# Attention into a multiplicative feed-forward network on one core: a half chunk's numerator and division placed elsewhere, and stores put behind the last transpose

## The chip, the cores and the metric

The kernel runs on one core of one Trainium2 chip. The metric is the device time of one execution in microseconds; the time before is the median of three runs. The engines are TensorE (PE in the profile; its weight loads are PEld), VectorE (DVE), ScalarE (ACT), GpSimd (POOL) and SyncE (SP). Transfers are issued by POOL (loads, and most stores), SP (transposes, and some stores) and ACT (the last stores).

## The reference

Eight batches of eight heads, 576 positions, head size 64. The first part is linear attention with cosine weights, the second a network that multiplies two projections.

```
phi(x) = concat(relu(x) * cos(theta), relu(x) * sin(theta))        # theta = pi/2 * position / 576
kv  = phi(k)^T v           z = sum over positions of phi(k)        # per batch and head
x   = (phi(q) kv) / (phi(q) z + 1e-6)                              # 4608 rows of 512
out = ((x w1) * (x w2)) w3 w_out                                   # w1, w2: 512 x 1024; w3: 1024 x 1024; w_out: 1024 x 512
```

## The kernel before, in words

**Tiles.** A batch has five chunks c of positions: 0 to 3 with 128 rows and chunk 4 with 64 (the "half chunk"). The 4608 rows of x make nine tiles t of 512 rows, so a tile takes chunks of two batches: tile 6 has batch 5's chunks 1 to 3 and batch 6's chunk 0; tile 7 has batch 6's chunks 1 to 4 and batch 7's half chunk; tile 8 has batch 7's chunks 0 to 3.

**The order is written out by hand.** `PLAN` (lines 26 to 259) is a text in which each line is a row of steps, and the loop at lines 1180 to 1183 issues them from the top down. Every engine, and every issuer of transfers, takes its own instructions in this order, one after another; a step that waits holds all that its engine has behind it. The words that matter here (b is the batch, c the chunk, t the tile; the last letter is the engine: V VectorE, A ScalarE, G GpSimd):

- `f t` is the next step of tile t's first stage, the products with w1 and w2 (`ffn_groups`, line 696, and for tiles 6 to 8 `fast_units`, line 832). For tiles 2 to 5 the same generator goes on with the output products (`seven_products`, line 1010). `o t` is the next step of the output products of tiles 6 to 8.
- `q b c n` makes the features of a query chunk: the cosine half on VectorE (L513), the sine half of the first n heads on ScalarE (L518), the other heads on VectorE (L521). `qd b c` transposes them into `qpT` by a DMA that SP issues (L542).
- `n b c` is the numerator with its denominator: eight products of 65 columns on TensorE (L605) into a pair of PSUM banks, `pnum`. `d b c` divides: `den` with the 1e-6 (L617 on ScalarE where the step says A, L619 on VectorE otherwise), a reciprocal (L620) and the product `xblk` (L621), both on VectorE. There are two pairs of `pnum` banks until the word `more` (line 193); from then on one, so a numerator waits until the division before it has read the bank. `xd b c` transposes `xblk` into its place in the tile's `xT` by a DMA that SP issues (L643).
- `xs t i` are four sums of x blocks for tiles 6 to 8 (L830); `h t p V` combines two partial results into abT (L890); `s t i V` are sums of abT blocks for the output products (L1008). All are on VectorE.
- `st` stores the oldest finished pair of 128-row blocks of the output through POOL, `ss` through SP. `sg` and `sx` do what `st` does behind a gate: a one-element copy on POOL (L432) that reads some tile and so waits until this tile is there. `sg` reads the newest `asb`, a copy that only the tiles before 6 make; `sx` reads the first column of the block that was transposed last in the plan's order. All later POOL work stands behind the gate.

A pair to be stored goes out as two or four transfers, depending on where its rows lie.

**Tiles 6 to 8** make their first stage with seven products in place of eight, in 14 steps for units 0 and 1. The steps are, as (unit, product): (0,1), (0,7) and (0,6) for each half, (0,4), (0,2), (0,5), (1,1), (0,3), (1,6), (1,7), (1,2), (1,4), (1,5), (1,3). For tile 6 these are the words `f 6` of lines 195, 197 to 208 and 211; lines 203 to 208 are (0,3) to (1,5). VectorE and ScalarE read the banks after each product: L862, L866, L869 and L877 are ScalarE's copies, L872, L881 and L884 VectorE's sums and products.

**The output products** of tiles 2 to 7 are also seven in place of eight (L1019): A11 B11 into a bank `u`, then s3 t3 into a bank `w`, and later products that are added into the same banks after ScalarE (L1030) or VectorE (L1027) has read them. In tiles 2 to 5 the product s2 t2 goes into `u` behind the copy of C11 by ScalarE, and s4 B22 goes into `u` behind VectorE's addition to C22. The second product into w's bank waits likewise for the copy of C22.

Around the edits:

```
136..141   f 3 twice, then: tile 3's last products (L705, abT L774), then its output products
186..196   tile 5's output products, with batch 6's numerators and divisions
202..217   tile 6's first stage and output products, with batch 7's numerators
218..237   tile 7, with batch 7's last divisions (line 225) and transposes (line 226), and the stores
```

Of the kernel before, what the change touches and what calls it, by code (L numbers as in the profile page):

```python
# [134 lines left out]
f 3  # L135
f 3
f 3; xd 3 2
f 3; lg 6 v 0; n 4 2; n 4 3; d 4 2 A; q 5 0 8; xd 4 1; q 5 3 8
f 3
f 3; xd 4 0; lx 6 q 0; lg 6 q 1  # L140
f 3; l 6 v 1; lg 6 k 0; v 6 1 G
f 3
f 3
# [42 lines left out]
f 5; q 7 0 8  # L186
f 5
f 5
f 5; n 6 0; xd 5 2; n 6 4; d 6 0 A; d 6 4 A; v 7 0 A
f 5  # L190
f 5; lg 7 k 1; lg 7 v 1; n 6 2; d 6 2 A; xd 6 0; v 7 4 G; xd 6 4
f 5
f 5; more
# [8 lines left out]
f 6; q 7 1 4; xd 6 2; sg; kv 7  # L202
f 6; q 7 3 8; h 6 0 V; s 6 3 V
f 6
f 6
f 6
f 6
f 6; n 7 4; h 6 1 V; qd 7 1
o 6; s 6 2 V; d 7 4 A
o 6  # L210
f 6; s 6 1 V; qd 7 3; s 6 4 V; n 7 3; xd 6 1; gx 0; d 7 3 A
o 6; sx; xd 6 3
# [13 lines left out]
f 7; xd 7 1  # L226
f 7; ss
f 7
f 7; h 7 1 V; s 7 2 V; xs 8 1 V; sg; s 7 1 V
o 7  # L230
f 7; s 7 4 V
o 7
# [982 lines left out]
```

## Time and profile before

| What | Value |
|---|---|
| time, median of 3 runs (lowest to highest) | 240.03 us (239.41 to 242.28) |
| the profiled execution's own time | 241.31 us |
| its span, first to last instruction | 239.5 us |
| TensorE busy | 230.4 us, 96% |
| VectorE, ScalarE, GpSimd busy | 193.1, 134.7, 88.6 us |
| granted TensorE clock | 1.000 |
| bytes moved | 40.51 MB, mean 169 GB/s |

The rows of the timeline are: start in us, duration in us, engine, line, operation, output tile <- input tiles, shapes, x how many instructions are merged in the row, and in brackets the engine's idle time ahead of the row with what ended it. A row is cut at the end of the window that was asked for. In the rows of the chain of waits stand start, duration, engine, tile, line and count. The rows of the table of windows give, for a stretch, the busy time of PE, PEld, DVE, ACT and POOL with the instructions in brackets, then the granted clock, the share of the DMA engines' time and GB/s. A row of DMA issues gives tiles, issuer, kind, count and the median time from issue to landing in us; "DMA to landing us min/median/max" is the same for all issues of one line.

### The profile page before, as it was taken

To read this page: it belongs to the slowest core of one execution; us is meant where nothing else is said; L and a number is where in the kernel's file an instruction comes from. 1 tells how busy PE (TensorE), PEld (TensorE's weight loads), DVE (VectorE), ACT (ScalarE), POOL (GpSimd) and SP (SyncE) were. 2 spreads that over 40 slices of the span, in tenths; PEclk is the share of its full clock that TensorE was granted. 3 is DMA by queue.
4 is the path that set the end of the run, shared out by engine and by line. 5 is a ranking of instruction groups with operands and counts; after the bars stand their busy time and mean duration, and the time that the engine had idled before them with its cause. 6 is when DMAs were issued, how large, how long until landed. Compare 5 with 4: busy or idle time off the path is not lost.

```text
span 239.5 us, 6014 instructions
## 1 busy us (share of the span) xinstructions
PE 230.4 (96%) x2316; PEld 170.6 (71%) x2316; DVE 193.1 (81%) x448; ACT 134.7 (56%) x250; POOL 88.6 (37%) x163
## 2 busy tenths in 40 slices
PE   8899999999999999999999999999999899999993
PEld 3479544475974596698668857984889788978872
DVE  6984595968888977999989479997979898894782
ACT  2754314597665833776556445767579437627730
POOL 8653878680903324130342212502271231920000
PEclk9999999999999999999999999999999999999999
DMA  6999999999999999999599997999988763999304
GB/s 190 196 197 198 167 192 170 197 196 196 178 192 152 134 155 194 177 138 192 71 156 181 193 217 98 122 185 193 145 142 203 107 186 69 231 297 265 112 16 160
DMA packets 86013, 40.51 MB, mean 169 GB/s; under 512 B 49632, under 2 KB 83424, under 8 KB 85984
## 3 DMA queue, kind: packets, MB, share of 16 engines
q0 software_dynamic: 39024, 24.65, 70.0%
q1 hardware_dynamic: 46672, 15.28, 39.1%
q8 instruction: 18, 0.29, 0.5%
q10 hardware_dynamic: 288, 0.20, 0.3%
q14 instruction: 11, 0.09, 0.1%
HBM read 38.80 MB, written 9.44 MB: 201 GB/s over the span
## 4 chain that ended last, share of the span: by engine, by line
PE 59%; DMA 26%; POOL 6%; DVE 3%; issue 2%; SPq 1%; ACT 1%; DVEq 0%; POOLq 0%; ACTq 0%
PE ffnps L705 23%; PE ffnps L1019 11%; PE ffnps L849 8%; DMA qs<-in_q_dram 7%; DMA kf<-in_k_dram 6%; PE ffnmore L849 6%; DMA w2b<-in_moe_w_dram 5%; DMA xT<-xblk 4%; PE pnum L605 3%; PE ffnps L789 3%; PE pnum L570 3%; DMA early<-in_moe_w_out_dram 3%; POOL early L420 2%; DMA qpT<-qp 2%; PE ffnps L951 1%
## 5 line engine op out<-in xcount | busy, mean ns | idle before, releaser
L705 PE MATMUL ffnps<-xT,w1b 128*128 128x256 bf16 (+2 forms) x320 | 51.5, 294 | 0.2
L705 PE MATMUL ffnps<-xT,w2b 128*128 128x256 bf16 (+2 forms) x320 | 51.5, 294 | 0.0
L705 PEld LDWEIGHTS <-w1b 128*128 128x128 bf16 x320 | 28.8, 98 | 12.1 <-issue 0.8
L705 PEld LDWEIGHTS <-w2b 128*128 128x128 bf16 x320 | 28.7, 98 | 11.7
L621 DVE TENSOR_TENSOR xblk<-pnum,den 128x512 bf16<-128x512 f32 (+1 forms) x38 | 26.3, 691 | 2.1 <-DVE den L620 0.2
L768 ACT CAST asb<-ffnps 128x512 bf16<-128x512 f32 x24 | 14.0, 584 | 19.1 <-PE ffnps L705 17.3
L518 ACT ACTIVATE kp<-kf,sinv 128x512 bf16<-128x512 bf16 (+5 forms) x33 | 21.1, 663 | 0.8 <-DMA kf<-in_k_dram 0.8
L1019 PEld LDWEIGHTS <-abT 128*128 128x128 bf16 x192 | 18.6, 98 | 3.6 <-DVE abT L774 0.6
L518 ACT ACTIVATE qp<-qs,sinv 128x512 bf16<-128x512 bf16 (+4 forms) x29 | 18.0, 643 | 3.5 <-issue 1.7
L774 DVE TENSOR_TENSOR abT<-asb,ffnps 128x512 bf16<-128x512 bf16 x24 | 16.1, 678 | 4.8 <-PE ffnps L705 4.0
L534 POOL COPY va<-vs 128x512 bf16<-128x512 bf16 (+1 forms) x15 | 9.9, 666 | 23.7 <-DMA vs<-in_v_dram 23.7
L605 PEld LDWEIGHTS <-qpT 128*128 128x128 bf16 x320 | 14.4, 98 | 5.9 <-issue 1.5
L432 POOL COPY seen<-asb 128x1 bf16<-128x1 bf16 x16 | 3.9, 246 | 35.9 <-ACT asb L768 18.9
L605 PE MATMUL pnum<-kvs,qpT 128*128 128x65 bf16 x304 | 15.4, 194 | 1.6 <-DVE xblk L621 1.3
L758 DVE TENSOR_TENSOR abT<-asb,ffnps 128x512 bf16<-128x512 bf16 x16 | 10.9, 684 | 6.6 <-PE ffnps L705 5.6
L1030 ACT COPY osb<-ffnps 128x512 f32<-128x512 f32 x16 | 9.2, 582 | 11.9 <-PE ffnps L1019 10.3
L789 PE MATMUL ffnps<-w34b,abT 128*128 128x512 bf16 x64 | 15.6, 379 | 0.0
L513 DVE TENSOR_SCALAR kp<-kf,cosv 128x512 bf16<-128x512 bf16 (+1 forms) x40 | 15.4, 397 | 0.2 <-DMA kf<-in_k_dram 0.2
L1019 PEld LDWEIGHTS <-s 128*128 128x128 bf16 x144 | 13.7, 98 | 1.9 <-DVE s L1008 0.3
L751 ACT CAST asb<-ffnps 128x512 bf16<-128x512 f32 x16 | 9.3, 583 | 9.5 <-PE ffnps L705 9.5
L490 PE MATMUL ffnps<-early,turned 128*128 128x512 bf16 x64 | 14.3, 379 | 0.0
L513 DVE TENSOR_SCALAR qp<-qs,cosv 128x512 bf16<-128x512 bf16 (+1 forms) x34 | 12.0, 373 | 1.6 <-DMA qs<-in_q_dram 1.5
(163 smaller groups left out, 484.4 us busy)
## 6 DMA issues: line engine op xcount, KB each, us to landing
kf<-in_k_dram POOLq DMA_DIRECT2D x7, 320.0 KB, 7.9
early<-in_moe_w_dram POOLq DMA_DIRECT2D x16, 128.0 KB, 5.5
out_dram<-osb SPq DMA_DIRECT2D x8, 256.0 KB, 3.4
vs<-in_v_dram POOLq DMA_DIRECT2D x6, 320.0 KB, 6.0
kf<-in_k_dram POOLq DMA_DIRECT2D x7, 256.0 KB, 7.5
qs<-in_q_dram POOLq DMA_DIRECT2D x5, 320.0 KB, 6.1
qs<-in_q_dram POOLq DMA_DIRECT2D x6, 256.0 KB, 6.7
vs<-in_v_dram POOLq DMA_DIRECT2D x6, 256.0 KB, 7.7
```

Of the source, the lines that this page charges most:

```text
L490: nc.tensor.matmul(acc[:, :], lhsT=w3T[:, lc, :], rhs=woutb[:, lc, :], start=(lc == 0), stop=(lc == 7))
L513: nc.vector.tensor_scalar(out=dst[:R, c, :, 0:D], in0=rows[:R], scalar1=0.0, scalar2=cosv[:R, at:at + 1], op0=ALU.max, op1=ALU.mult)
L518: nc.scalar.activation(out=dst[:R, c, 0:n, D:F], in_=rows[:R, 0:n], func=ACTF.Relu, scale=sinv[:R, at:at + 1], bias=0.0)
L605: nc.tensor.matmul(nt[:, h // 4, ds((h % 4) * 65, 65)], lhsT=qpT[:, h, ds(at, 128)], rhs=kvs[:, h, :], start=True, stop=True)
L621: nc.vector.tensor_tensor(out=xblk[rows, g0:g0 + ng], in0=n4[:, :, :, 0:D], in1=den[rows, 0:ng].unsqueeze(3).to_broadcast([R, ng, 4, D]), ...
L705: nc.tensor.matmul(out, lhsT=w[:, kc, ts(jc, 128)], rhs=x[:, kc, tok], start=(first and kc == 0), stop=(kc == 3), skip_group_check=not first)
L758: nc.vector.tensor_mul(out=abT[:, ts(pair, 2), ts(half, 256)], in0=asb[:].rearrange("p (i n) -> p i n", i=2), in1=bT[:, :].rearrange("p (i ...
L768: nc.scalar.copy(out=asb[:], in_=aT[:, :])
L774: nc.vector.tensor_mul(out=abT[:, jc, :], in0=asb[:], in1=bT[:, :])
L789: nc.tensor.matmul(ops[:, :], lhsT=abT[:, jc, ts(ms, 128)], rhs=w34b[:, jc, :], start=(jc == 0), stop=(jc == 7))
L849: nc.tensor.matmul(into[:, ts(i, 256)], lhsT=w[:, kc, ts(2 * u + i, 128)], rhs=a[:, kc, :], start=(first and i == 0 and kc == 0), stop=(i ...
L1019: nc.tensor.matmul(into[:, ts(ms, 256)], lhsT=a[:, kc, ts(ms, 128)], rhs=b[:, kc, :], start=(first and ms == 0 and kc == 0), stop=(ms == 1 ...
```

## The change

Six lines of the plan become others; no function is touched.

```
-f 3; lg 6 v 0; n 4 2; n 4 3; d 4 2 A; q 5 0 8; xd 4 1; q 5 3 8
+f 3; lg 6 v 0; n 4 2; n 4 3; d 4 2 A; xd 4 1
 f 3
-f 3; xd 4 0; lx 6 q 0; lg 6 q 1
+f 3; q 5 0 8; q 5 3 8; xd 4 0; lx 6 q 0; lg 6 q 1
...
-f 5; n 6 0; xd 5 2; n 6 4; d 6 0 A; d 6 4 A; v 7 0 A
-f 5
+f 5; n 6 0; xd 5 2; d 6 0 A; v 7 0 A
+f 5; n 6 4; d 6 4 A
...
 f 6
+f 6; n 7 4; d 7 4 A
 f 6
 f 6
-f 6
-f 6; n 7 4; h 6 1 V; qd 7 1
-o 6; s 6 2 V; d 7 4 A
+f 6; h 6 1 V; qd 7 1
+o 6; s 6 2 V
...
-f 7; h 7 1 V; s 7 2 V; xs 8 1 V; sg; s 7 1 V
+f 7; h 7 1 V; s 7 2 V; xs 8 1 V; sx; s 7 1 V
```

1. Lines 138 and 140: the features of batch 5's chunks 0 and 3 are issued two lines later, behind tile 3's last pair of products and the first half of its first output product.
2. Lines 189 and 190: numerator and division of batch 6's half chunk are issued one step of tile 5's output products later; the copy `v 7 0` on ScalarE then comes ahead of the half chunk's `den`.
3. Lines 205 to 209: numerator and division of batch 7's half chunk are issued behind step (1,7) of tile 6, where the numerator stood behind (1,5) and the division behind the first output product and the sum `s 6 2`.
4. Line 229: the store that was gated by the newest `asb` is gated by the block transposed last in the plan's order, `xd 7 1` of line 226. The gate holds what POOL has behind it: this store (two transfers), the store of line 233 (four) and that of line 237 (two).

## The prediction

> **What bounds the kernel now.** I read the page's busy rows first, then the last steps of the chain of waits, then TensorE's timeline for rows that state an idle time, and around each of these the timelines of the other engines.
>
> ```profile
> span 239.5 us, 6014 instructions
> PE 230.4 (96%) x2316; PEld 170.6 (71%) x2316; DVE 193.1 (81%) x448; ACT 134.7 (56%) x250; POOL 88.6 (37%) x163
> ...
> 230.06 1.73 PE ffnps L951 x8
> ...
> 233.97 1.76 PE ffnps L951 x16
> ```
>
> TensorE (PE) is busy 96% of the span, and its products stand at the end of the chain, up to 235.73. So the change is worth what it takes from PE's idle time, and nothing else. From 65 us on, four rows of PE name an idle time and its releaser; I quote each with the row ahead of it.
>
> ```profile
> 124.51 0.49 PE L1019 MATMUL ffnps<-w34b,abT 128*128 128x256 bf16 x3
> 125.35 0.72 PE L1019 MATMUL ffnps<-w34b,abT 128*128 128x256 bf16 x5 [0.35 <-DVE abT L774]
> ...
> 168.26 0.42 PE L605 MATMUL pnum<-kvs,qpT 128*128 128x65 bf16 x8
> 168.96 0.42 PE L605 MATMUL pnum<-kvs,qpT 128*128 128x65 bf16 x8 [0.28 <-DMA qpT<-qp]
> ...
> 189.05 1.04 PE L1019 MATMUL ffnps<-early,s 128*128 128x256 bf16 x8
> 189.92 1.04 PE L849 MATMUL ffnps<-va,w2b 128*128 128x256 bf16 x8
> 191.85 0.42 PE L605 MATMUL pnum<-kvs,qpT 128*128 128x65 bf16 x8 [0.90 <-DVE xblk L621]
> 192.11 1.03 PE L1019 MATMUL ffnps<-early,s 128*128 128x256 bf16 x8
> ...
> 214.31 1.04 PE L1019 MATMUL ffnmore<-w34b,abT 128*128 128x256 bf16 x8
> 215.62 0.61 PE L849 MATMUL ffnps<-xT,w1b 128*128 128x256 bf16 x4 [0.28 <-DMA xT<-xblk]
> ```
>
> The bracket counts from the modelled end of a pipelined product. What is lost is counted better from starts: eight products of 256 columns take 0.87 (189.05 to 189.92), a numerator takes 0.26 (191.85 to 192.11). So 125.35 was due at 124.51 + 3/8 x 0.87 = 124.84 (0.51 lost), 168.96 at 168.52 (0.44), 191.85 at 190.79 (1.06), 215.62 at 215.18 (0.44). Together 2.45 us, 1.0% of the time: even the whole of it lies within the 2% that a measurement of this kernel can tell from no change. The four edits aim at these four waits, one each. What counts is what is late next.
>
> **Edit 1, two query features of batch 5 behind tile 3's last product.** Nothing is added or removed. Before, VectorE sat until the query load had landed, made both cosine halves, and only then multiplied the last abT for which PE waits.
>
> ```profile
> 123.97 1.33 ACT L518 ACTIVATE qp<-qs,sinv 128x512 bf16<-128x512 bf16 x2 [1.68 <-issue]
> 123.98 0.72 DVE L513 TENSOR_SCALAR qp<-qs,cosv 128x512 bf16<-128x512 bf16 x2 [0.67 <-DMA qs<-in_q_dram]
> 124.62 0.67 DVE L774 TENSOR_TENSOR abT<-asb,ffnps 128x512 bf16<-128x512 bf16 x1
> 125.22 1.05 ACT L1030 COPY osb<-ffnps 128x512 f32<-128x512 f32 x2
> 125.91 1.04 PE L1019 MATMUL ffnps<-early,s 128*128 128x256 bf16 x8
> ```
>
> After, L774 starts at 123.98 at the latest, where VectorE was free for the features, ends 0.67 later, and the product at 124.84 waits no more. But the sine halves are in ScalarE's order too, and the new line still puts them ahead of the copy of C11, which comes with the next `f 3`. ScalarE waits for the same load, copies C11 from 125.22 to about 125.8 (half of the 1.05 row, each copy overlapping the next), and the product at 125.91 accumulates into the bank that this copy reads. PE would now be there at 125.91 - 0.51 = 125.40 and waits until about 125.85 to 125.95. **Worth 0**; from both sides: -0.51 if that bank does not hold it, +0.1 if the copy's release is slow. The features' transposes on SP stand 15 lines further on in the plan; xd 4 1, which moves ahead of the features in the plan, is on SP and behind a division that is done in either order.
>
> **Edit 2, batch 6's half chunk one step on.** PE runs the 0.87 step first, so the transposed query that it waited for at 168.96 has landed when the numerator comes at 169.39. No instruction is added.
>
> ```profile
> 169.94 0.69 DVE L621 TENSOR_TENSOR xblk<-pnum,den 128x512 bf16<-128x512 f32 x1
> 173.29 1.43 DVE L1027 TENSOR_TENSOR early<-ffnps,early 128x512 f32<-128x512 f32 x2
> 174.78 1.03 PE L1019 MATMUL ffnps<-w34b,s 128*128 128x256 bf16 x8
> ```
>
> VectorE's order does not change by this edit (division of chunk 0, of chunk 4, addition, division of chunk 2, two additions), and the first division starts at 169.94 and the last two additions end at 173.29 + 1.43 = 174.72, with a fifth of a microsecond of idle time between. The product at 174.78 adds into the bank that the last of these additions reads. PE comes 0.44 earlier to the numerator of chunk 2, which needs chunk 0's bank (169.94 + 0.69 = 170.63, so a pause of some 0.2), and again 0.2 earlier to 174.78, where it waits for VectorE. **Worth 0**; -0.44 if VectorE runs ahead after all, +0.1 if the chunk's den, now behind another copy on ScalarE, delays the division.
>
> **Edit 3, batch 7's half chunk three steps sooner.** Before, numerator 7 4 was issued right ahead of tile 6's first output product, its division behind six VectorE instructions, and numerator 7 3 needs the same single bank.
>
> ```profile
> 185.15 1.09 ACT L866 COPY kf<-ffnmore 128x512 f32<-128x512 f32 x2
> 185.30 1.04 PE L849 MATMUL ffnps<-xT,w1b 128*128 128x256 bf16 x8
> 186.88 1.29 DVE L872 TENSOR_TENSOR s<-ffnmore,vs 128x512 bf16<-128x512 f32 x2 [0.61 <-PE ffnmore L849]
> 190.12 0.69 DVE L1008 TENSOR_TENSOR s<-abT,s 128x1024 bf16<-128x1024 bf16 x1
> 190.73 0.19 DVE L620 RECIPROCAL den<-den 64x8 f32<-64x8 f32 x1
> 191.02 0.68 DVE L621 TENSOR_TENSOR xblk<-pnum,den 64x512 bf16<-64x512 f32 x1
> 191.63 1.27 DVE L884 TENSOR_TENSOR abT<-asb,ffnps 128x512 bf16<-128x512 bf16 x2
> 196.72 0.75 DVE L830 TENSOR_TENSOR va<-xT 128x512 bf16<-128x512 bf16 x2
> 197.61 0.60 PE L849 MATMUL ffnmore<-va,q0f 128*128 128x256 bf16 x4
> ```
>
> After: numerator at 185.30, ScalarE's den behind its two copies (185.15 + 1.09 = 186.24) to about 186.3, VectorE free since 186.88 - 0.61 = 186.27, so reciprocal 186.31, division 186.60 (0.29 later, as 190.73 to 191.02), so the sums L872 start at 186.60 + 0.61 = 187.21 (0.61 as 191.02 to 191.63) instead of 186.88. The s of 190.12 then ends at 190.81 + 0.33 = 191.14, and L884 follows at once, at 191.06 instead of 191.63: VectorE gains **0.57**, the pause filled. PE issues numerator 7 3 at 190.79 without a wait and the product with s at about 191.2, not 192.11: 0.9 gained there. But down the line PE needs x sums that VectorE makes in unbroken order from 191.63 on: the second L830 ended at 196.72 + 0.75 = 197.47, and the product that reads it came at 197.61. That moves by VectorE's 0.57, so of PE's 0.9 about **0.6** stays. Bounds: 0 (the division meets other work) to -1.06 (the whole wait).
>
> **Edit 4, `sg` to `sx`.** The old gate read an asb of tile 5, long there, so nothing held the stores. The new gate reads the last transposed x block, 7 1, and all later stores of POOL stand behind it: two, four and, from line 237, two.
>
> ```profile
> 202.70 3.12 POOL L683 DMA_DIRECT2D out_dram<-osb  x6 [0.28 <-issue]
> 207.16 2.99 SPq L643 DMA_TRANSPOSE xT<-xblk  x1
> ...
> xT<-xblk SPq DMA_TRANSPOSE x1, 2.7
> xT<-xblk SPq DMA_TRANSPOSE x1, 8.4
> ```
>
> The last two rows are issue to landing of single transposes, one issued between 198.5 and 200 (2.7), before POOL's stores, and that of 207.16, amid them (8.4). After, 7 1 is issued at 207.16 - 0.6 = 206.6 with only the six stores of 202.70 and transpose 7 0 ahead; between 2.7 and 8.4 I take 5, landing at 211.6. PE wants it at 215.18 - 0.6 = 214.6. The wait goes: **-0.44**. At worst the landing keeps its 8.4 (215.0) and nothing of the 0.44 is won. Behind 214.6, the chain that follows is PE's own.
>
> The cover of the later stores: they now leave from 211.6 on, against SP's own last ones.
>
> ```profile
> 218.00:222.00 4.00, 4.00 (x38) 3.47 (x37) 2.00 (x4) 3.19 (x7) 0.00 (x0) 1.00 0.92 243
> 226.00:230.00 4.00, 4.00 (x37) 3.40 (x36) 3.04 (x5) 2.02 (x5) 0.00 (x0) 1.00 0.03 6
> ```
>
> Between 226 and 230 the DMA engines stood idle (share 0.03). A held pair of rows is 128 x 2 x 512 values of 4 bytes, 0.5 MB; three pairs go by POOL and four by SP: 3.5 MB at 243 GB/s is 14.4 us, from 211.6 to 226, and tile 8's first store comes behind the product that ends at 230.06 + 1.73 - 1.04, about 231. The Trainium skill, "DMA: Bandwidth & Descriptors", section "Issuing engines are not separate DMA queues", speaks against the edit: transfers of all issuers share the same 16 engines, so holding back POOL's stores takes none away and meets SP's later ones. The 8.4 beside the 2.7 agrees; by that rule the edit is worth the same as long as the pile is gone by 231, and less if not, which is the fourth rival.
>
> **The sum.** 0 + 0 - 0.6 - 0.44 = -1.04. The profiled execution took 241.31 around its span of 239.5; it would take 240.3. It was slower than the median of the three runs, 240.03, and I apply the same difference there: **239.0 us**.
>
> **Rivals.** (a) Edits 1 and 2 pay too, because the bank of C11 or VectorE's row of work gives way: up to 0.95 more, 238.0. For it: PE's rows name just these releasers. Against: the two releases above, each within 0.15 of PE's start. (b) Edit 4 does not do what it says, the landing keeps its 8.4, held by the stores of 202.70: 0.6 alone, 239.4. (c) The 0.6 and the 0.44 both vanish, VectorE losing elsewhere what it gains in the pause: 240.0; against it stands that VectorE's row from 186.88 to 191.63 has no other idle time. (d) The stores' pile reaches tile 8's stores; that begins where 3.5 MB move at less than 3.5 / (231 - 211.6), 180 GB/s; at 150 it ends 23.3 us after 211.6, at 234.9, some 4 us late on the first of those stores, perhaps 2 on the end: 241.0. (e) Slower: numerator 7 4 now stands three steps nearer to its transposed query.
>
> ```profile
> 179.84 1.66 SPq L542 DMA_TRANSPOSE qpT<-qp  x1
> ...
> qpT<-qp SPq DMA_TRANSPOSE x1, 4.8
> ...
> DMA to landing us min/median/max: 3.3/4.8/7.4
> ```
>
> It was issued at 179.84 and landed at 184.64; PE asks at 185.30. With the 7.4 that the slowest of these takes it lands at 187.24, PE stands 1.94 (all its later work is queued behind), and 1.94 - 1.04 gives +0.9, 240.9. It decides from a landing of 185.30 + 1.04 = 186.34 on, 6.5 after the issue. For it: stores run beside it. Against: they do so now.
>
> **Chances.** Forecast 0.62; (a) 0.12; (b) 0.11; (c) 0.07; (d) 0.02; (e) 0.06. The forecast's own range is 238.6 to 239.5; (a), (b) and (c) stretch it to 237.9 to 240.3, with about 0.1 outside. None of the cases reaches 2%: within 2% 0.96, 0.02 on either side for what I have not seen.
>
> **What would show it.** Right: no idle time of PE at L605 behind the L849 of tile 6; numerator 7 4 between two L849 groups, its division in VectorE's row ahead of L872; L872 about 0.3 later, L884 about 0.6 sooner; the L1019 with s after ScalarE's copy of C11 near 125.9 still; the landing of transpose 7 1 under 6 us and no wait for xT; POOL's stores behind 211. Wrong: a gain at 125 or 169 that lasts, a wait for xT at tile 8's first product, or numerator 7 4 waiting for qpT.

## The result, and the profile after

| | before | after |
|---|---|---|
| median of 21 runs each, taken side by side | 241.46 us (239.41 to 244.34) | 239.06 us (238.09 to 241.00) |
| ratio | | 0.992, interval 0.9897 to 0.9943 |
| profiled execution, its span | 241.31, 239.5 us | 239.04, 237.2 us |
| TensorE busy | 230.4 us | 230.3 us |

The ratio makes 241.46 x 0.008 = 1.93 us, between 1.38 and 2.49. The ratio compares means and leaves out two executions of the kernel before, 243.04 and 244.34, which lie over 1.5% above its fastest; the medians count them. So the kernel became faster by more than the forecast's 1.04, which lies below this interval. That the forecast's 239.0 stands so near to 239.06 is partly chance: the three runs that it started from had a median 1.43 below that of the 21. And the prediction had held that a change within 2% can't be told from none; with 21 runs on either side this one, 0.8%, is told from none.

The page of the kernel after, its span and busy row:

```profile
span 237.2 us, 6014 instructions
PE 230.3 (97%) x2316; PEld 170.7 (72%) x2316; DVE 192.7 (81%) x448; ACT 134.5 (57%) x250; POOL 88.0 (37%) x163
```

The work is the same, so the 2.3 us of span came out of TensorE's idle time. From 100 us on no row of TensorE names an idle time any more. Not all of the 2.3 is the change's, though: tile 2's first output product started at 99.94 before and at 99.25 after, 0.69 sooner, ahead of all four edits. Over the fourteen profiled executions, whatever the kernel, this start lies between 98.21 and 99.94. The other 1.6 came at the four places of the edits: there TensorE lost 0.51, 0.51, 1.18 and 0.44 before and 0.22, 0.36, 0.48 and 0 after, 1.58 less. How much of that is the edits' own, and how much a transfer that landed earlier, is for the experiments.

The four places in turn, in the timeline of the kernel after. **Edit 1**, TensorE, VectorE and ScalarE around the last products of tile 3:

```profile
123.06 1.33 ACT L518 ACTIVATE qp<-qs,sinv 128x512 bf16<-128x512 bf16 x2 [1.46 <-issue]
124.30 1.05 ACT L1030 COPY osb<-ffnps 128x512 f32<-128x512 f32 x2
124.91 1.03 PE L1019 MATMUL ffnps<-early,s 128*128 128x256 bf16 x8
```

The query load landed at 122.99, the two sine halves start at once, the copy of C11 stands behind them and ends its first half near 124.9, and the product that adds into that bank starts at 124.91, 0.22 after it was due. The wait for abT is gone; what is left of it is the copy's.

**Edit 2**, TensorE and VectorE around the numerator of batch 6's half chunk:

```profile
168.66 1.04 PE L1019 MATMUL ffnps<-w34b,abT 128*128 128x256 bf16 x8
168.95 0.69 DVE L621 TENSOR_TENSOR xblk<-pnum,den 128x512 bf16<-128x512 f32 x1
169.79 0.42 PE L605 MATMUL pnum<-kvs,qpT 128*128 128x65 bf16 x8
172.30 1.28 DVE L1027 TENSOR_TENSOR early<-ffnps,early 128x512 f32<-128x512 f32 x2
172.66 1.04 PE L849 MATMUL ffnmore<-xT,w1b 128*128 128x256 bf16 x8
173.63 1.03 PE L1019 MATMUL ffnps<-w34b,s 128*128 128x256 bf16 x8
```

The numerator of chunk 2 was due at 168.66 + 0.87 = 169.53 and starts 0.26 later, behind the division of chunk 0 (168.95 + 0.69 = 169.64). The product at 173.63 was due at 173.53, 0.10 lost, behind the second addition (172.30 + 1.28 = 173.58). Both now wait for VectorE, 0.36 together.

**Edit 3**. Times of the two executions compare best against one product that stands ahead of the edit, the L849 with va and q0f: 184.42 before, 183.28 after, so 1.14 is to be added.

```profile
183.28 1.04 PE L849 MATMUL ffnmore<-va,q0f 128*128 128x256 bf16 x8
184.15 0.42 PE L605 MATMUL pnum<-kvs,qpT 128*128 128x65 bf16 x8
184.95 0.19 ACT L617 ACTIVATE den<-pnum 64x8 f32<-64x8 f32 x1
185.17 0.20 DVE L620 RECIPROCAL den<-den 64x8 f32<-64x8 f32 x1
185.47 0.68 DVE L621 TENSOR_TENSOR xblk<-pnum,den 64x512 bf16<-64x512 f32 x1
186.08 1.27 DVE L872 TENSOR_TENSOR s<-ffnmore,vs 128x512 bf16<-128x512 f32 x2
189.92 1.28 DVE L884 TENSOR_TENSOR abT<-asb,ffnps 128x512 bf16<-128x512 bf16 x2
190.06 1.05 PE L1019 MATMUL ffnps<-early,s 128*128 128x256 bf16 x8
195.82 0.60 PE L849 MATMUL ffnmore<-va,q0f 128*128 128x256 bf16 x4
```

The division sits in VectorE's pause, ahead of L872. With the 1.14, L872 starts at 187.22 (before 186.88, 0.34 later), L884 at 191.06 (before 191.63, 0.57 sooner), the product with s at 191.20 (before 192.11, 0.91 sooner) and the product that reads the x sums at 196.96 (before 197.61, 0.65 sooner). Of the 0.91, then, 0.06 goes in the products from 190.06 to 192.74 (2.68 us, 2.62 before) and 0.21 in a wait at 195.82; 0.06 comes back at 198.07, where TensorE waits less than before, and by 199 the gain is 0.70.

**Edit 4**, transposes, gate, stores and tile 8's first product:

```profile
202.99 4.76 SPq L643 DMA_TRANSPOSE xT<-xblk  x2
210.36 0.41 POOL L432 COPY seen<-xT 128x1 bf16<-128x1 bf16 x1 [6.09 <-DMA xT<-xblk]
210.88 3.18 POOL L683 DMA_DIRECT2D out_dram<-early  x6
212.47 1.04 PE L1019 MATMUL ffnmore<-w34b,abT 128*128 128x256 bf16 x8
213.34 0.60 PE L849 MATMUL ffnps<-xT,w1b 128*128 128x256 bf16 x4
214.18 1.03 POOL L683 DMA_DIRECT2D out_dram<-early  x2
...
xT<-xblk SPq DMA_TRANSPOSE x1, 4.9
```

The second transpose of the first row, 7 1, was issued at 205.38 and landed at 210.24, in 4.9 us where it had taken 8.4. TensorE asks for it 8.0 us after the issue, before (215.18 - 207.16) and after (213.34 - 205.38), so it comes 3.1 early where it came 0.4 late. The gate opens on it and all eight later stores of POOL leave behind 210.88. Tile 8's first product starts 0.87 after the product ahead of it, with nothing lost. The end is as before: the last of the piled stores lands at 223.29 and tile 8's first store is issued at 230.14, and the table of windows shows the load falling (the last two columns are the share of the DMA engines' time and GB/s).

```profile
212.00:220.00 8.00, 8.00 (x74) 7.06 (x73) 5.39 (x11) 4.67 (x9) 3.18 (x7) 1.00 0.93 294
220.00:228.00 8.00, 8.00 (x72) 6.83 (x70) 6.27 (x12) 4.84 (x10) 0.00 (x0) 1.00 0.30 85
```

### The profile page after: what moved, and what is told of

Its sections match the earlier page's. It is cut to its first block, busy times and chain, and to the rows that moved or that the text cites. A ratio compares the mean times of both kernels' runs of the same rounds, so it can differ in the third digit from the quotient of the medians.

```text
span 237.2 us, 6014 instructions
## 1 busy us (share of the span) xinstructions
PE 230.3 (97%) x2316; PEld 170.7 (72%) x2316; DVE 192.7 (81%) x448; ACT 134.5 (57%) x250; POOL 88.0 (37%) x163
## 4 chain that ended last, share of the span: by engine, by line
PE 63%; DMA 21%; POOL 8%; DVE 3%; issue 2%; ACT 1%; DVEq 0%; POOLq 0%; SPq 0%
PE ffnps L705 26%; PE ffnps L1019 12%; PE ffnps L849 7%; DMA kf<-in_k_dram 7%; DMA qs<-in_q_dram 6%; PE ffnmore L849 6%; DMA w2b<-in_moe_w_dram 5%; POOL early L420 3%; PE ffnps L789 3%; PE pnum L605 3%; PE pnum L570 3%; PE ffnps L951 1%; DMA xT<-xblk 1%; DMA out_dram<-osb 1%; PE ffnps L941 1%
## 5 line engine op out<-in xcount | busy, mean ns | idle before, releaser
L534 POOL COPY va<-vs 128x512 bf16<-128x512 bf16 (+1 forms) x15 | 9.4, 633 | 25.0 <-DMA vs<-in_v_dram 25.0
L605 PEld LDWEIGHTS <-qpT 128*128 128x128 bf16 x320 | 14.5, 98 | 4.2 <-DVE xblk L621 0.7
L432 POOL COPY seen<-asb 128x1 bf16<-128x1 bf16 x15 | 4.4, 295 | 32.9 <-ACT asb L768 16.4
L513 DVE TENSOR_SCALAR kp<-kf,cosv 128x512 bf16<-128x512 bf16 (+1 forms) x40 | 14.6, 377 | 0.5 <-DMA kf<-in_k_dram 0.5
L513 DVE TENSOR_SCALAR qp<-qs,cosv 128x512 bf16<-128x512 bf16 (+1 forms) x34 | 13.0, 401 | 0.8 <-DMA qs<-in_q_dram 0.8
```

The costliest lines, as they stand in the source:

```text
L513: nc.vector.tensor_scalar(out=dst[:R, c, :, 0:D], in0=rows[:R], scalar1=0.0, scalar2=cosv[:R, at:at + 1], op0=ALU.max, op1=ALU.mult)
L605: nc.tensor.matmul(nt[:, h // 4, ds((h % 4) * 65, 65)], lhsT=qpT[:, h, ds(at, 128)], rhs=kvs[:, h, :], start=True, stop=True)
```

## The experiments

Each was timed against the kernel before on the same chip. The theory of the prediction: edits 1 and 2 are worth nothing, because ScalarE's order and VectorE's row of work hold TensorE right behind; edits 3 and 4 carry the gain. The rival: a wait that was named in one execution is not the wait of every execution, and a transfer that lands late in one may land early in the next. What is "lost" is counted from start to start of TensorE's products, as in the prediction. Three profiles (e3, the run of edit 3 alone, xs_first, that of the reordered x sums, and e123, that of all but edit 4) hold a stall near 105 us, ahead of all four edits (last section); of their traces only what is named is used, and the other eleven are called undisturbed.

**The kernel before, unchanged, once more.**

> The kernel before, unchanged, as a measure of what varies by itself. Theory: the start of the numerator that ends the load phase (60.04 us in the profile before, 59.25 in the one after the change) moves by several tenths of a microsecond from one execution to the next with no edit at all, while the four waits of TensorE behind it stay: 0.4 to 0.55 near 125, 0.3 to 0.5 near 169, 1.0 to 1.1 near 191, 0.3 to 0.5 near 215. Rival: the load phase is steady, within 0.2 us of 60.04, and the 0.79 gained there in the profile after the change belongs to the change. The ratio holds 1.

Measured: 0.9999 (0.9968 to 1.003). TensorE around three of the four places:

```profile
167.63 0.42 PE L605 MATMUL pnum<-kvs,qpT 128*128 128x65 bf16 x8
168.99 0.42 PE L605 MATMUL pnum<-kvs,qpT 128*128 128x65 bf16 x8 [0.94 <-DMA qpT<-qp]
191.88 0.42 PE L605 MATMUL pnum<-kvs,qpT 128*128 128x65 bf16 x8 [0.89 <-DVE xblk L621]
215.93 0.61 PE L849 MATMUL ffnps<-xT,w1b 128*128 128x256 bf16 x4 [0.55 <-DMA xT<-xblk]
```

There is no wait near 125 at all. At 168.99 1.10 is lost (due at 167.63 + 0.26), where the first profile showed 0.44. At 191.88 it is 1.06, to the hundredth what the first profile showed. At tile 8 it is 0.72 where it was 0.44. So my theory that all four waits stay did not hold. Of the four waits on which the prediction's sum rests, only the one that no transfer releases is a constant of the kernel. The numerator that ends the load phase came at 59.88, only 0.16 from 60.04, so this run alone does not settle where the 0.79 belongs; but in the runs of edits 3 and 4 together and of edit 4 alone, which touch nothing up to there, tile 2's first output product starts at 98.57 and 99.02, against 99.94 and 99.83 in the two executions of the kernel before. That part moves without an edit.

**Edits 3 and 4 alone**, the two that were to carry everything.

```
 f 6
+f 6; n 7 4; d 7 4 A
 f 6
 f 6
-f 6
-f 6; n 7 4; h 6 1 V; qd 7 1
-o 6; s 6 2 V; d 7 4 A
+f 6; h 6 1 V; qd 7 1
+o 6; s 6 2 V
...
-f 7; h 7 1 V; s 7 2 V; xs 8 1 V; sg; s 7 1 V
+f 7; h 7 1 V; s 7 2 V; xs 8 1 V; sx; s 7 1 V
```

> Edits 3 and 4 alone (batch 7's half chunk, and the gate of the stores). Theory: these two carry nearly all of the gain; against the kernel before TensorE loses 1.06 + 0.12 - 0.15 - 0.21 - 0.07 = 0.75 us less around 191 to 199 and 0.44 less at tile 8's first product, 1.2 us in all (ratio 0.995), while the waits near 125 and 169 stay as they were. Rival: they bring 0.6 + 0.44 = 1.04 as forecast and the rest of the measured 1.9 us is in edits 1 and 2 (ratio 0.996 here, 0.996 there).

Measured: 0.996 (0.9925 to 0.9995). At 191 to 199 and at tile 8 it is the kernel after: 0.48 and nothing lost. Near 125 stands the largest wait of this kind of all profiles, 0.74 lost, and at 169 to 174 0.48. By the ratio the half that was to carry all carries half of the 0.008, but the interval reaches 0.9925, nearly all of it, so the times do not decide. The traces of all runs, added up further down, give these two edits about three quarters.

```profile
125.65 0.72 PE L1019 MATMUL ffnps<-w34b,abT 128*128 128x256 bf16 x5 [0.57 <-DVE abT L774]
```

**Edit 1 alone.**

```
-f 3; lg 6 v 0; n 4 2; n 4 3; d 4 2 A; q 5 0 8; xd 4 1; q 5 3 8
+f 3; lg 6 v 0; n 4 2; n 4 3; d 4 2 A; xd 4 1
 f 3
-f 3; xd 4 0; lx 6 q 0; lg 6 q 1
+f 3; q 5 0 8; q 5 3 8; xd 4 0; lx 6 q 0; lg 6 q 1
```

> Edit 1 alone (two query features of batch 5 two lines later). Theory: TensorE's wait moves from the product that needs the last abT to the product that adds into the bank which ScalarE's copy of C11 reads; its start stays tied to the landing of the query load, about 1.9 us behind it where it was 2.0, so 0.1 us is gained at an equal landing, and less wait shows only where the load lands sooner. Ratio 1.000. Rival: the wait is gone, 0.5 us less near 125, ratio 0.998.

Measured: 1.0006 (0.9976 to 1.0036). Nothing was lost near 125, the load having landed early, as in the kernel before when it was profiled again; so this profile alone can't say what the edit saves, and the times say nothing. The same profile has the longest wait at tile 8, 1.81 lost, its transpose landing 9.79 after its issue, with not one edit there:

```profile
215.56 0.61 PE L849 MATMUL ffnps<-xT,w1b 128*128 128x256 bf16 x4 [1.65 <-DMA xT<-xblk]
```

**Edit 2 alone.**

```
-f 5; n 6 0; xd 5 2; n 6 4; d 6 0 A; d 6 4 A; v 7 0 A
-f 5
+f 5; n 6 0; xd 5 2; d 6 0 A; v 7 0 A
+f 5; n 6 4; d 6 4 A
```

> Edit 2 alone (batch 6's half chunk one step later). Theory: the wait of 0.44 on the transposed query goes, 0.2 to 0.3 of it comes back at chunk 2's numerator, behind VectorE's division of chunk 0, and up to 0.1 at the product behind VectorE's last addition; 0.15 us is gained, ratio 0.999. Rival: the whole 0.44 to 0.51 is gained and no wait takes its place, ratio 0.998.

Measured: 0.9965 (0.9936 to 0.9994), 0.84 us, with an interval that leaves no change out, just. In its trace the numerator still waits for the transposed query, one step later than before, since this one landed 5.4 us after its issue (2.8 to 5.4 over the undisturbed profiles):

```profile
169.01 0.42 PE L605 MATMUL pnum<-kvs,qpT 128*128 128x65 bf16 x8 [0.28 <-DMA qpT<-qp]
```

**Edit 3 alone, and edit 4 alone**: of the diff of edits 3 and 4 above, the lines from `f 6` to `o 6` alone, and the line of `f 7` alone.

> Edit 3 alone (batch 7's half chunk three steps sooner). Theory: the wait of 1.06 behind the division goes; TensorE waits 0.15 at the product with s and 0.2 at the first product of tile 7 that reads an x sum, both held by VectorE's order, so 0.6 to 0.75 us is gained by 199. With the old gate the last transpose still lands some 8 us after its issue, issue and landing move with the division, so the wait for xT at tile 8 stays at 0.3 to 0.6. Ratio 0.997. Rival: the wait for xT grows by all that was gained, because the landing is set by the stores and not by the issue: ratio 1.000.

> Edit 4 alone (the store gate). Theory: the last transposed x block lands 4 to 6 us after its issue, not 8.4, tile 8's first product waits no more, 0.44 us is gained, nothing is lost at the end: ratio 0.998. The wait of 1.06 near 191 stays. Rival: the stores, now later, make the end longer or the landing keeps its 8 us; ratio 1.000 or above.

Measured: 0.9976 (0.9942 to 1.0009) for edit 3 and 0.997 (0.9941 to 1.0) for edit 4. Edit 4's trace keeps 1.06 lost at 191 and has nothing lost at tile 8 (landing in 5.09). Edit 3's, where I expected 0.3 to 0.6 lost at tile 8, has nothing lost there either, with the old gate:

```profile
217.79 1.04 PE L1019 MATMUL ffnmore<-w34b,abT 128*128 128x256 bf16 x8
218.66 0.60 PE L849 MATMUL ffnps<-xT,w1b 128*128 128x256 bf16 x4
```

Its transpose landed 7.71 after the issue, just inside the 8.0 at which TensorE asks for it. It is one of the three disturbed profiles, but it shows that the old gate does not always cost something. The four single edits add up to 0.0006 - 0.0035 - 0.0024 - 0.0030 = -0.0083, beside -0.008 for the whole; each term is uncertain by 0.003, so this fits, and proves little.

**All but edit 4**: the whole change with line 229 as it was.

```
-f 7; h 7 1 V; s 7 2 V; xs 8 1 V; sx; s 7 1 V
+f 7; h 7 1 V; s 7 2 V; xs 8 1 V; sg; s 7 1 V
```

> The changed kernel without edit 4, the old gate in its place. Theory: the last transpose of x lands 7.7 to 9.8 us after its issue, as in all runs with the old gate, where the new gate gave 4.6 to 5.2; issue and landing move with the division, so TensorE waits 0 to 1.5 us at tile 8's first product, and the kernel is 0.4 to 1 us slower than the changed one: ratio 0.995 to 0.996. Rival: the landing follows the earlier issue closely enough that edit 4 brings nothing once edit 3 is made: no wait, ratio 0.992.

Measured: 0.995 (0.9915 to 0.9985), 0.003 above the whole change, as edit 4 alone gives it, though the two intervals overlap; the transpose landed 8.74 after its issue and tile 8 lost 0.82.

**What holds TensorE near 125 once edit 1 is made?** By the prediction it is the copy of C11 behind the sine halves. First, the change with the features behind both copies:

```
-f 3; q 5 0 8; q 5 3 8; xd 4 0; lx 6 q 0; lg 6 q 1
+f 3; xd 4 0; lx 6 q 0; lg 6 q 1
...
-f 3
+f 3; q 5 0 8; q 5 3 8
```

> All four edits, and the two query features of edit 1 placed two lines further still, behind the copies of C11 and C22 in ScalarE's order. Theory: ScalarE's sine halves, which wait for the load, held the copy of C11 and with it TensorE's product near 125; now no wait is there (under 0.05 us), 0.2 to 0.45 us less than the changed kernel. Rival: the product is held by something else (VectorE's sum s2, the bank of the copy of C22), a wait of 0.2 or more stays near 125 or comes within the next 3 us.

Measured: 0.9904 (0.9867 to 0.9941), and nothing lost near 125. Since the load varies by itself, I then made it late, with the features where the change has them and again with them behind the copies:

```
-f 3; lg 5 q 0; lt 5 q 1; kv 4; k 5 1; d 3 3 V; k 5 4; v 5 4 V
+f 3; lg 5 q 0; kv 4; k 5 1; d 3 3 V; k 5 4; v 5 4 V
...
-f 3; n 4 0; d 4 0 V; n 4 1; d 4 1 V
+f 3; lg 5 q 1; n 4 0; d 4 0 V; n 4 1; d 4 1 V
```

> All four edits, and the second part of batch 5's query load issued two lines later, behind the asb copy of tile 3's next step, so that it lands some 1 to 2 us later. Theory: ScalarE's sine halves wait for this load and hold the copy of C11, so TensorE's wait at the product s2 t2 grows one for one, to 1 to 2.2 us near 125; the start of this product stays about 1.9 us behind the landing. Rival: VectorE's order alone set the wait before the change, edit 1 has cured it, and the later landing costs under 0.3 us.  Ratio 0.997 by the theory, 0.992 by the rival.

> The same later load, and the two query features behind the copies of C11 and C22, as in the run that placed them there. Theory: the copy of C11 no longer stands behind the load, so there is no wait over 0.1 us at the product s2 t2 however late the load lands; ratio 0.991. Rival: the load holds TensorE by another way (a shared bank, VectorE's cosine halves), and 0.5 us or more is lost within 3 us of that product.

Measured: 0.9956 (0.9917 to 0.9994) and 0.9891 (0.9825 to 0.9958). The load was issued 2.6 later than in the kernel after (118.93 against 116.30) but landed only 0.45 later, at 123.44, for it took 4.5 where it had taken 6.7. So the wait that I expected at 1 or more came out at 0.50; its place and its releaser are as expected. The late load with the features where the change has them:

```profile
123.52 1.33 ACT L518 ACTIVATE qp<-qs,sinv 128x512 bf16<-128x512 bf16 x2 [1.74 <-issue]
124.76 1.05 ACT L1030 COPY osb<-ffnps 128x512 f32<-128x512 f32 x2
125.37 1.03 PE L1019 MATMUL ffnps<-early,s 128*128 128x256 bf16 x8 [0.34 <-ACT osb L1030]
```

and with the features behind the copies:

```profile
122.96 0.59 ACT L1030 COPY osb<-ffnps 128x512 f32<-128x512 f32 x1 [1.54 <-PE ffnps L1019]
124.32 1.33 ACT L518 ACTIVATE qp<-qs,sinv 128x512 bf16<-128x512 bf16 x2
124.51 1.04 PE L1019 MATMUL ffnps<-early,s 128*128 128x256 bf16 x8
```

In the first the product comes 125.37 - 123.44 = 1.93 behind the landing, in the kernel after 124.91 - 122.99 = 1.92: load, two sine halves, copy, product. Without edit 1, in the three executions that waited, it comes 125.91 - 123.90 = 2.01 (before), 126.20 - 124.24 = 1.96 (edits 3 and 4) and 125.09 - 123.16 = 1.93 (edit 2), by the cosine halves and abT or by the same copy, whichever ends later. So at an equal landing edit 1 saves 0 to 0.1. In the second profile the copies run ahead of the sine halves, and the product comes 124.51 - 122.87 = 1.64 behind the landing with nothing lost. In the next run, which has the features behind the copies too, it comes 123.66 - 122.45 = 1.21 behind it, still with nothing lost; the chain of 1.92 would have cost 0.7 there.

**Is the rest at 169 to 174 VectorE's?** The change, the features behind the copies, and batch 6's half chunk behind everything else:

```
-f 5; n 6 4; d 6 4 A
-f 5; lg 7 k 1; lg 7 v 1; n 6 2; d 6 2 A; xd 6 0; v 7 4 G; xd 6 4
 f 5
+f 5; lg 7 k 1; lg 7 v 1; n 6 2; d 6 2 A; xd 6 0; v 7 4 G
+f 5; n 6 4; d 6 4 A; xd 6 4
```

> All four edits, the two query features behind the copies of C11 and C22, and batch 6's half chunk (numerator, division, transpose) behind chunk 2's numerator and one more step of tile 5. Theory: VectorE has the same work ahead of the addition that frees the bank of the product s4 B22, so what TensorE no longer waits at the numerators (0.26 at chunk 2's, and what the transposed query costs) it waits at that product: 0.35 us in all near 169 to 175, as in the executions of edit 2 in which the query had landed; against the runs in which it had not (0.51) 0.15 is gained. Ratio 0.991. Rival: TensorE's waits there fall under 0.2 us in all.

Measured: 0.9913 (0.9882 to 0.9943). The numerators no longer wait, and TensorE stands 0.50 at the product behind VectorE's addition instead, where I had expected 0.35:

```profile
170.16 0.20 DVE L620 RECIPROCAL den<-den 64x8 f32<-64x8 f32 x1 [0.17 <-ACT den L617]
171.17 1.29 DVE L1027 TENSOR_TENSOR early<-ffnps,early 128x512 f32<-128x512 f32 x2
172.51 1.03 PE L1019 MATMUL ffnps<-w34b,s 128*128 128x256 bf16 x8 [0.33 <-DVE early L1027]
```

So what the numerators no longer wait is lost again behind VectorE's row, as the theory had it. It is 0.15 more than expected; in this order VectorE itself stands 0.17 for ScalarE's `den` of the half chunk, which is about as much. The same trace shows 0.20 lost at numerator 7 4, which waited for its transposed query: the mechanism of rival (e), at a tenth of its price.

**Can more of edit 3's 0.9 be kept?** The change, with the sum `xs 7 3` ahead of `xs 7 1` in line 215, since the first of tile 7's x sums that TensorE asks for is not the first that VectorE makes.

```
-o 6; xd 7 4; n 7 2; xs 7 1 V; xs 7 3 V; xs 7 2 V; xs 7 4 V
+o 6; xd 7 4; n 7 2; xs 7 3 V; xs 7 1 V; xs 7 2 V; xs 7 4 V
```

> All four edits, and tile 7's third x sum ahead of its first in VectorE's order. Theory: of the time that edit 3 frees, 0.2 us was lost at tile 7's first product with an x sum, because VectorE makes that sum second; made first it is there 0.33 us sooner and the wait of 0.21 goes, with no wait at the product with the second sum 0.44 us later. Rival: the product waits for another thing (the bank, the addition before the sums), and the wait stays.

Measured: 0.9938 (0.9909 to 0.9966). The wait at the first product with an x sum is gone, and one of 0.23 stands at the next product, which reads the second sum. My theory that the order of these sums costs 0.2 fell: the wait moved one product on, and with the sums in this order nothing is gained. That VectorE as a whole is late there fits this, but no other order was tried.

No version can be told from the changed kernel: 0.9904, 0.9891 and 0.9913 all have intervals that reach over 0.992. By the traces, the features behind the copies are the better place: no wait near 125 came in the three profiles that have them there.

## Why the prediction was right in direction and short in size

What TensorE lost at each place, in us, over the undisturbed profiles, in the order of the sections above (e1 to e4 are the runs of one edit alone, e34 that of edits 3 and 4; sine_late has the features behind the copies, load_late the late load, load_sine_late both):

| place | without the edit: before; same; others | mean | with the edit: after; others | mean | difference |
|---|---|---|---|---|---|
| 125, edit 1 | 0.51; 0; e34 0.74, e2 0.21, e4 0 | 0.29 | 0.22; e1 0, load as it was | 0.11 | about 0.2 |
| 169 to 174, edit 2 | 0.51; 1.17; e34 0.48, e1 0.35, e4 1.14 | 0.73 | 0.36; e2 0.51, sine_late 0.51, load_late 0.35, load_sine_late 0.36 | 0.42 | 0.31 |
| 191 to 199, edit 3 | 1.18 in each | 1.18 | 0.48 in each | 0.48 | 0.70 |
| tile 8, edit 4 | 0.44; 0.72; e1 1.81, e2 0.82 | 0.95 | 0 in each | 0 | 0.95 |

The differences sum to 0.2 + 0.31 + 0.70 + 0.95 = 2.2, beside the measured 1.93 (1.38 to 2.49). With the disturbed profiles of edit 3 alone (0) and of all but edit 4 (0.82) counted too, tile 8 has a mean of 0.77 without edit 4, and the sum is 2.0.

- **Edit 1, worth 0.** The step held. The wait for VectorE's abT went, and ScalarE's copy of C11 behind the sine halves took its place, 0.22 after and 0.50 with the load made late; where the features stand behind the copies it is gone. The 0.2 of the table rests on two profiles with the edit, in which the load landed earlier than in four of the five without it; at an equal landing the edit saves 0 to 0.1, and alone it gave 1.0006.
- **Edit 2, worth 0.** This step failed, and a gain at 169 that lasts is among the signs of being wrong that the prediction names. I held that VectorE's row, with a fifth of a microsecond of idle time in it, fixed when TensorE could go on. But the row of two additions, 1.43 before, is 1.28 after: 0.15 of it was the second addition's wait for TensorE, inside a merged row. And the 0.44 of that one execution was a small sample of a wait that was 1.10 in the next. VectorE's floor is real, 0.35 to 0.36 in the four profiles with the least loss; what lies above it depends on the landing of the transposed query. Where this took 2.8 to 3.4 us, 0.35 was lost with the edit and without it; where it took about 4.1, 0.51 and 0.48 without and 0.36 with it; where it took 5.2 to 5.4, 1.17 and 1.14 without and 0.36 to 0.51 with it.
- **Edit 3, 0.6.** Right at each step: L872 0.34 later (0.33 forecast), L884 0.57 sooner (0.57), the product with s 0.91 sooner (0.9), the x sums' product 0.65 sooner (0.6). Summed to 199 it is 0.70. No transfer is part of it, and every profile of the table gives the same to 0.01.
- **Edit 4, 0.44.** The mechanism was right and the size short by half. The landing was put at 5 and took 4.6 to 5.2 in the eight kernels with the edit that were profiled; the wait went in all of them. But what it saves is what the old gate loses, and that is what the landing takes beyond some 8.0: 0 at 7.71, 0.44 at 8.41, 0.72 at 8.68, 0.82 at 8.74 and 8.79, 1.81 at 9.79. The execution that I read had the second shortest of these six.
- **The rivals.** (a) came half true, by edit 2. (b), (c) and (d) are refuted: the landing fell, the trace of edits 3 and 4 together shows both gains at once, and POOL's and SP's stores had landed by 223.29, with the DMA engines at 0.30 between 220 and 228. The Trainium skill, "DMA: Bandwidth & Descriptors", section "Issuing engines are not separate DMA queues", has transfers of all issuers run on the same DMA engines, from which the prediction took that the held stores meet SP's later ones. They do, at a share of 0.93 from 212 to 220, and in this trace TensorE waits for none of it. (e) did not come in the kernel after: the transposed query landed at 183.61 and was wanted at 184.15.

So the sum was made to the hundredth from one execution, and of the 2.45 us of lost time that it priced, 0.51 + 0.44 + 0.44 = 1.39 hung on the landing of a transfer. With the second profile of the kernel before alone, by the same steps, edit 4 would have stood at 0.72, edit 2 at 1.17 less VectorE's floor, and at 125 there would have been no wait to price.

Open: the times can't price the edits one by one. Edit 2's 0.3 from the traces and its 0.84 (0.14 to 1.5) from the times agree only within that interval, and the means of the traces rest on two to six executions each.

## What to carry to other kernels

Here a wait that a transfer releases had a spread (0 to 1.81 us at one place), one that engines release nearly none (1.18 each time): profile the kernel a few times before a wait on a landing is priced, and look for the time at which the landing begins to matter. When the wait of an engine is taken away, look for the next thing that the same late input releases, on every engine that shares it: here the load near 125 reached TensorE by VectorE and by ScalarE, and only moving both took the wait away. And a merged row whose duration is more than its instructions take by themselves hides a wait.

## What the runs showed of the hardware

**The same transpose takes 1.8 times as long beside POOL's later stores.** The last transpose of x took 4.6 to 5.2 us, in the mean 5.0, from issue to landing in eight profiles in which POOL's later stores were held back, and 7.7 to 9.8, in the mean 8.7, in six in which they were not; six stores of POOL and two transposes went ahead of it in either case. The transpose issued before those six stores took 2.5 to 3.1. In two executions of the kernel before, the transposed query of edit 2 took 4.1 and 5.4.

**A late transpose can cost TensorE its clock.** Three profiles, of kernels with different edits, have one stall near 105. In that of edit 3 alone, the chain in the timelines of VectorE, ScalarE and TensorE, and the time to landing of the transposed queries between 84 and 108:

```profile
104.05 0.88 DVE L513 TENSOR_SCALAR qp<-qs,cosv 128x512 bf16<-128x512 bf16 x3 [2.35 <-DMA qpT<-qp]
104.68 1.05 ACT L1030 COPY osb<-ffnps 128x512 f32<-128x512 f32 x2
105.30 1.82 PE L1019 MATMUL ffnps<-early,s 128*128 128x256 bf16 x8 [3.61 <-ACT osb L1030]
106.91 1.91 PE L1019 MATMUL ffnps<-early,abT 128*128 128x256 bf16 x8
...
DMA to landing us min/median/max: 5.6/9.3/14.5
```

Features wait for a transpose that still reads their buffer, the copy behind them on ScalarE waits too, and TensorE stands 3.6 us. That transpose, issued near 90, took 13.3 to 14.5 us in the three profiles and 8.0 to 11.0 in the others. Then eight products take 1.6 to 1.7 where they take 0.87 (105.30, 106.91, and the next row at 108.61). The third figure from the end in the windows is the granted clock.

```profile
105.00:106.00 1.00, 0.70 (x4) 0.55 (x4) 0.89 (x2) 1.00 (x3) 0.00 (x0) 0.69 1.37 193
106.00:107.00 1.00, 1.00 (x7) 0.70 (x5) 0.00 (x0) 1.00 (x3) 0.00 (x0) 0.50 1.76 189
107.00:108.00 1.00, 1.00 (x7) 0.69 (x6) 0.00 (x0) 0.94 (x2) 0.00 (x0) 0.50 1.53 96
108.00:109.00 1.00, 1.00 (x7) 0.76 (x6) 0.07 (x1) 0.00 (x0) 0.00 (x0) 0.60 1.25 173
109.00:110.00 1.00, 1.00 (x11) 0.90 (x10) 0.62 (x1) 0.22 (x1) 0.00 (x0) 1.00 1.42 188
```

If the clock is either whole or half, these windows make 0.62 + 1 + 1 + 0.8 = 3.4 us at half, and then it comes back. The Trainium skill, "TensorE: Matmul & The Clock Gate", section "What's actually happening", has it so: an idle window of some 3.4 us halves the clock, and a busy one as long gives it back. The 3.4 us at half agree. The stalls agree only roughly: they were 3.6, 3.5 and 3.1 us, the last of them shorter than the page's window. Elsewhere in these three traces, from 8 us on, no wait of TensorE reached 1 us and the clock stayed at 1.00. A stall is not the only way there, though: in the second profile of the kernel before, the clock was 0.50 from 13 to 16 us, in the load phase, though from 8 us on TensorE had waited at most 0.6 at a time.
